# A gated linear recurrence with a maxout FFN: the two tiles of a group come from two sequences instead of two neighbouring stretches of one

## The chip, the core and the metric

The kernel runs on one core of a Trainium2 chip. The core has five engines that work side by side, each with its own queue of instructions: TensorE (PE in the profile, its weight loads PEld), VectorE (DVE), ScalarE (ACT), GpSimd (POOL) and SyncE (SP), which here only issues DMAs. The metric is the device time in microseconds. Before the change it is 688.7 us, the median of three runs (688.65 to 689.51).

## The reference

Four sequences (B = 4) of 768 tokens, with 8 heads of 48 dimensions, go through a recurrence with a complex gate, and then through a feed-forward layer:

```python
mag = np.sqrt(a_re * a_re + a_im * a_im)
scale = np.minimum(mag, 0.999) / (mag + 1e-06)
a_re_n, a_im_n = (a_re * scale, a_im * scale)
...
for t in range(S):
    new_re = ar * S_re - ai * S_im
    new_im = ar * S_im + ai * S_re
    S_re, S_im = (new_re + kv, new_im)
    y[:, :, t] = np.einsum('bhd,bhde->bhe', q[:, :, t], S_re)
...
h = np.maximum(np.maximum(x @ w1, x @ w2), x @ w3)
return (h @ w_out).astype(np.float32)
```

The state S is zero at the start of each sequence, and the sequences do not depend on each other. The FFN works on each of the 3072 tokens by itself (384 to 768 and back). All data are float32.

## The kernel before

**Tiles and groups.** A tile x holds 128 tokens of one sequence, all heads (24 tiles, six per sequence). A group g is C = 2 tiles, which share the work on the gates: 12 groups. Before the change the two tiles of a group are neighbours in one sequence (`GB` = 3 groups per sequence), and tile x follows tile x-1. A tile has two chunks of 64 tokens.

**The gates** (`gate_steps`, `turns`, `sines`, `products`). Instead of running the recurrence token by token, the kernel writes the gate as a size and an angle, sums the logarithms of the size and the angles along the tokens, and multiplies k and q by what the sums give. The step s0 squares (L350, L351) and adds (L352, L353), s1 ends with `Ln`, the logarithm of the size (L362 on ACT, then L363 on DVE), and s2 makes the tangent of half the angle in `w`; L373, on POOL from group 2 on, is one of its products. `turns` takes Arctan of `w` and adds what is missing of the angle (L390, L391). The matmuls `cs` then sum the angles over the tokens of a tile: with the triangular matrix `upto` for the tile's own tokens, and for the second tile of a group also with the matrix of ones `every`, which adds the sum over the first tile. The result is rounded to whole turns (`t`, L403, on ACT) and reduced (`nf`, L405, on DVE), and its cosine and sine (`af`, L419, then `CS`, on ACT) multiply k and q (`uk`, `uq`, L469). The angle at the end of a group is carried to the next: two DMAs on ACT's queue (L413) copy the last row of the second tile's `nf` to the tile `carry`, and in the next group a POOL operation (L381) subtracts it from the first row of `ai`, which L391 adds in. A group at the head of a sequence gets no carry.

**The states.** `state(x)` computes `dk`, the sum of outer products of k and v for both chunks of a tile (32 matmuls, 64 records in the profile, since each float32 matmul has two), and from it the state ahead of the tile's second chunk and ahead of the next tile. The states lie in the tiles `g`, of which there are two. Tile 0 of a sequence has its first state set to zero by POOL (L592) and its second copied from `dk` (L614); elsewhere a state is multiplied by a decay (L616) and `dk` is added (L617). `prep` multiplies k and q by decay factors (L517); its last part makes `QG`, by which the state is read. `scores` makes the products `A` and `B`, `gather` picks from them into `atm` (L564), and `outputs` sums `y` from `atm` and v (inside the chunk) and from `QG` and `g` (from the state ahead of it).

**The FFN.** `up_step` multiplies 256 tokens by a third of the features of one of w1, w2, w3; the first result goes to `hT` by a copy on ACT (L657), the two others by a maximum on DVE (L659). `out_step` multiplies by w_out, and SP's queue stores.

**Order.** All PSUM results use one pool of four tiles (two banks each), handed out as they come free: a new result waits until what was in its tile four results before has been read. Groups 0 and 1 are woven from lists of steps; from group 2 on, `group` calls the steps in an order that is written out, and each matmul is tied to the one before it (`chained`), so that PE's order is that of the source. ACT's activations that need a table are tied to each other in the same way. For everything else the order on an engine is settled when the program is built, by priority and by what is expected to be ready; an engine then works through its queue in that order. In `group(g)` the angles of group g+1 are summed in the middle:

```python
outputs(x, tokens(x))
rest(y)
turning()
pairs(y)
units[0]()
units[1]()
for f in later:
    f()
feed(2)
turned(y + 1)
```

`turning` is `angles` of group g+1, with `feed(2)` inside (two steps of the FFN ahead of the sums); `pairs(y)` is `A`, `B` and their gathers, `units` make `uk` and `uq`, `later` is s0 and s1 of group g+2, and `turned` begins with the transposes `tp`, then `cut` (`F`) and `state` (`dk`).

Of the kernel before, what the change touches and what calls it, by code (L numbers as in the profile page):

```python
# [50 lines left out]
def kernel(  # L51
# [13 lines left out]
    nc = tc.nc  # L65
# [9 lines left out]
    W = C * DM  # L75
    TG = C * P
    NS = S // P
    GB = NS // C
    NG = B * GB
    NX = NG * C  # L80
    HU = 4

# [64 lines left out]
    def ones(name, *shape):  # L147
        t = const.tile([P, *shape], FP, name=name)
        nc.vector.memset(t, 1.0)
        return t  # L150
# [3 lines left out]
        keep(view, -low - 1, [[-s, n] for s, n in lp], 1)  # L154
        keep(view, high, [[s, n] for s, n in hp], -1)

    every = ones("every", L64)

    upto = ones("upto", P)

# [11 lines left out]


    vbs = [const.tile([P, 2, H // 2, P], FP, name="vb%d" % i) for i in range(4)]
    gs = [const.tile([P, 2, H // 2, P], FP, name="g%d" % i) for i in range(2)]
    atms = [const.tile([P, H, L64], FP, name="atm%d" % i) for i in range(2)]

    us = {nm: [const.tile([P, H, 2, L64], FP, name="u%s%d" % (nm, i)) for i in range(n)] for nm, n in (("k", 3), ("q", 2))}
# [56 lines left out]


    def rows(a, g, c, lo=0, n=P):
        b, s = divmod(g, GB)
        t0 = (s * C + c) * P + lo
        return a[b, :, t0:t0 + n, :].rearrange("h t d -> t h d")  # L240

    def load_a(g, c):
        for nm, src in (("ar", a_re), ("ai", a_im)):
# [3 lines left out]

    def halves(a, g, c, j):

        b, s = divmod(g, GB)  # L250
        t0 = (s * C + c) * P
        return a[b, j * 4:(j + 1) * 4, t0:t0 + P, :].rearrange("h (c t) d -> t c h d", c=2)

    def load_kq(g, c):
        for nm, src in (("k", k), ("q", q)):
# [81 lines left out]
    def gate_steps(g, cs):  # L337
        lo, hi = cs[0] * DM, (cs[-1] + 1) * DM

        def part(nm):  # L340
            t = T[nm, g]
            return (flat(t) if len(t.shape) == 4 else t)[:, lo:hi]

        def s0():
            if lo == 0:
                for nm in "Lwe":
                    T[nm, g] = nat1.tile([P, W], FP, tag=nm, name=nm)
                T["Ln", g] = nat2.tile([P, W], FP, tag="Ln", name="Ln")
            L, w, ar, ai = part("L"), part("w"), part("ar"), part("ai")
            nc.scalar.activation(out=w, in_=ar, func=AF.Square)  # L350
            nc.scalar.activation(out=L, in_=ai, func=AF.Square)  # L351
            nc.vector.tensor_tensor(out=L, in0=L, in1=w, op=OP.add)  # L352
            nc.vector.tensor_scalar(out=L, in0=L, scalar1=SMALL, scalar2=LARGE, op0=OP.max, op1=OP.min)  # L353
            act(out=L, in_=L, func=AF.Ln)

        def s1():

            L, w, e = part("L"), part("w"), part("e")
            act(out=w, in_=L, func=AF.Exp, scale=0.5)
            act(out=e, in_=L, func=AF.Exp, scale=-0.5)  # L360
            act(out=e, in_=e, func=AF.Ln, scale=1e-6, bias=1.0)
            nc.scalar.activation(out=L, in_=L, func=AF.Relu, scale=-0.5, bias=lnmax)  # L362
            nc.vector.scalar_tensor_tensor(out=part("Ln"), in0=L, scalar=-LNMAX, in1=e, op0=OP.add, op1=OP.add)  # L363

        def s2():

            L, w, e, ar, ai = part("L"), part("w"), part("e"), part("ar"), part("ai")
            nc.scalar.activation(out=e, in_=ar, func=AF.Abs)
            nc.vector.tensor_tensor(out=w, in0=w, in1=e, op=OP.add)
            act(out=L, in_=w, func=AF.Ln)  # L370
            act(out=L, in_=L, func=AF.Exp, scale=-1.0)

            (nc.gpsimd if g > 1 else nc.vector).tensor_tensor(out=ai, in0=ai, in1=L, op=OP.mult)  # L373
            nc.vector.tensor_tensor(out=w, in0=w, in1=L, op=OP.mult)
            nc.vector.scalar_tensor_tensor(out=w, in0=w, scalar=2.0, in1=ai, op0=OP.subtract, op1=OP.mult)

            nc.scalar.activation(out=ar, in_=ar, func=AF.Sign, bias=tiny)  # L377
            nc.scalar.activation(out=ai, in_=ar, func=AF.Copy, scale=-0.25, bias=0.25)
            nc.scalar.activation(out=ar, in_=ar, func=AF.Copy, scale=-1.0 / math.pi)
            if lo == 0 and g % GB > 0:  # L380
                nc.gpsimd.tensor_tensor(out=ai[0:1, 0:DM], in0=ai[0:1, 0:DM], in1=T["carry", g], op=OP.subtract)  # L381

        return [s0, s1, s2]

    def turns(g, cs, meanwhile):

        lo, hi = cs[0] * DM, (cs[-1] + 1) * DM
        w, ar, ai = T["w", g], flat(T["ar", g]), flat(T["ai", g])
        act(out=w[:, lo:hi], in_=w[:, lo:hi], func=AF.Arctan)
        nc.vector.tensor_tensor(out=w[:, lo:hi], in0=w[:, lo:hi], in1=ar[:, lo:hi], op=OP.mult)  # L390
        nc.vector.tensor_tensor(out=w[:, lo:hi], in0=w[:, lo:hi], in1=ai[:, lo:hi], op=OP.add)  # L391
        meanwhile(2)
        for c in cs:
            ps = banks("cs", DM)

            for ch in range(2):
                for n, mat in enumerate((upto[:, ch * L64:(ch + 1) * L64], every)[0:c + 1]):
                    for j in range(2):
                        at = (c - n) * DM + j * HC
                        mm(out=ps[j * L64:(j + 1) * L64, ch * HC:(ch + 1) * HC], lhsT=mat,  # L400
                           rhs=w[:, at:at + HC], start=n == 0, stop=n == c)
            t = nat2.tile([P, DM], FP, tag="t", name="t")
            nc.scalar.activation(out=t, in_=ps, func=AF.Copy, bias=MAGIC)  # L403
            nf = nat2.tile([P, DM], FP, tag="nf", name="nf")
            nc.vector.scalar_tensor_tensor(out=nf, in0=t, scalar=MAGIC, in1=ps, op0=OP.subtract, op1=OP.subtract)  # L405
            T["nf", g * C + c] = nf
            if g == 0:
                sines(g, [c])
            if c == C - 1 and (g + 1) % GB > 0:
                T["carry", g + 1] = nat1.tile([1, DM], FP, tag="carry", name="carry")  # L410
                for j in range(2):
                    last = (j + 1) * L64
                    nc.scalar.dma_start(out=T["carry", g + 1][:, j * HC:(j + 1) * HC], in_=nf[last - 1:last, HC:])  # L413

    def sines(g, cs):
        for c in cs:
# [94 lines left out]
    def prep(x, part):  # L511
        K, Q, F = T["K", x][0:DD], T["Q", x][0:DD], T["F", x][0:DD]

        def times(out, in_, c, n):

            f = F.rearrange("p s j n -> p (s j) n")[:, :, c:c + n].rearrange("p g (n e) -> p g n e", e=1)
            nc.vector.tensor_tensor(out=out, in0=in_, in1=f.to_broadcast([DD, 2 * H, n, 8]), op=OP.mult)  # L517

        def rows8(t):

            return t.rearrange("p g (n e) -> p g n e", e=8)

        base = Q[:, :, 0:32]
        if part == 0:
            q8 = rows8(Q[:, :, 32:48])
            times(q8, base.rearrange("p g (n u e) -> p g n u e", u=2, e=8)[:, :, :, 1], C8, 4)
            times(q8, q8, C8B, 4)
        elif part == 1:

            times(*(rows8(t.rearrange("p s (j t) -> p (s j) t", j=2)[:, :, 0:48]) for t in (KB[0:DD], K)), CK, 6)  # L530

            QB = un1.tile([P, 2 * H, 96], FP, tag="QB", name="QB")
            T["KB", x], T["QB", x] = KB, QB
            ends = QB[0:DD].rearrange("p g (s u e) -> p g s u e", s=6, e=8)[:, :, 0::5]
            times(ends, rows8(base[:, :, 16:32]), C16, 4)
        elif part == 2:
            src = Q.rearrange("p (g j) t -> p g j t", j=2)[:, :, 1:2, 0:32].to_broadcast([DD, 2 * H, 2, 32])
            times(T["QB", x][0:DD, :, 16:80].rearrange("p g (i n e) -> p g i n e", i=2, e=8),
                  src.rearrange("p g i (n e) -> p g i n e", e=8), C32, 8)
        else:  # L540
            QG = un1.tile([P, 2 * H, L64], FP, tag="QG", name="QG")
            times(rows8(QG[0:DD]), rows8(base), CG, 8)
            T["QG", x] = QG

    def scores(x, nm):
# [40 lines left out]

    def state(x):

        s = x % NS
        T["G", x] = gs[x % 2]  # L590
        if s == 0:
            nc.gpsimd.memset(T["G", x][0:DD, 0], 0.0)  # L592


        ps = banks("dk")
        for n in range(H):
            ch, i = divmod(n, 4)
            for j in range(2):
                r, o = slice(j * L64, (j + 1) * L64), i % 2 * (P - D)
# [9 lines left out]
            return heads(t).rearrange("p (j i) u d -> p j i u d", j=2)  # L609

        for c in range(2 if s < NS - 1 else 1):
            new = four(G[0:DD, 1] if c == 0 else gs[(x + 1) % 2][0:DD, 0])
            if s + c == 0:
                nc.vector.tensor_copy(out=new, in_=dk[:, c])  # L614
                continue
# [3 lines left out]
    def outputs(x, xs):  # L619
# [4 lines left out]
        for r in range(DM // 32):  # L624
            i, w = divmod(r, 3)
            runs = ((0,), (1, 2), (3,))[w]
            for c in range(2):
                todo = [(n, new) for new in (True, False) for n in runs]
                queues[r % 4] += [(r, c, i, n, new, (n, new) == todo[0], (n, new) == todo[-1]) for n, new in todo]
        for todo in zip(*queues):  # L630
            for r, c, i, n, new, start, stop in todo:
# [29 lines left out]
    def out_step(xs, x):  # L661
# [3 lines left out]
            mm(out=ps, lhsT=hT[:, f, o:o + P], rhs=wo[:, f], start=(f == 0), stop=(f == KF - 1))  # L665
        ot = fp2.tile([P, DM], FP, tag="ot", name="ot")
        nc.scalar.copy(out=ot, in_=ps)
        nc.sync.dma_start(out=out[x * P:(x + 1) * P, :], in_=ot)


    def call(f, *a):
# [192 lines left out]
```

## Time and profile before

One execution was profiled. Its time is 688.34 us and the span in the profile 686.6 us.

| what | value |
|---|---|
| time, median of 3 runs | 688.7 us |
| time of the profiled execution, and its span | 688.34 us, 686.6 us |
| mean granted TensorE clock | 0.974 |
| `up` matmuls, busy | 294.3 us |
| `op` matmuls, busy | 98.6 us |
| `y` matmuls, busy | 46.7 and 46.1 us |
| `cs` matmuls with `upto`, with `every`, busy | 22.9 us (192 records), 13.1 us (96) |
| `dk` matmuls, busy | 27.0 us (1536 records) |
| chain of waits, share of PE and of ACT | 69%, 11% |
| carry copies on ACT's queue, issue | 16 of 504 to 1875 ns, median 566 ns; 2.0 to 4.5 us to landing |

How to read it: a busy time is the time in which the engine had an instruction of that group under way. Matmuls overlap, so their rows add up to more than the time they take. In rows by time, the two numbers in front are start and duration, "x12" is the number of records taken together, and what stands in brackets is the idle time of the engine ahead of the instruction with what ended it. "ACTq" is the queue of ACT, which issues DMAs. "L117" is the helper that records every matmul; matmuls are told apart by the tile that they write.

### The profile page before, as it was taken

What the parts mean: (1) busy time and instruction counts of PE and PEld (TensorE: products, weight loads), DVE (VectorE), ACT (ScalarE), POOL (GpSimd) and SP (SyncE); (2) the same over time, 40 slices, a digit from 0 to 9 for tenths busy, and PEclk for the clock granted to TensorE, in tenths of its full rate; (3) what the DMA queues carried; (4) which work ended last, traced back from release to release, by engine and by line L of the source; (5) the groups of instructions that cost most, each with busy time, mean ns of one, the idle gap of its engine ahead of it and who ended that gap; (6) DMA issues with size and microseconds to landing.
All of it is one profiled execution on the core that took longest, in us unless ns stands there. A gap on an engine that the chain in (4) does not pass through costs nothing.

```text
span 686.6 us, 25182 instructions
## 1 busy us (share of the span) xinstructions
PE 613.9 (89%) x11196; PEld 505.9 (74%) x11196; DVE 492.1 (72%) x676; ACT 389.6 (57%) x617; POOL 116.3 (17%) x128
## 2 busy tenths in 40 slices
PE   1263396898999999999999999999999999999997
PEld 0162395887878878878878878878878788887785
DVE  4899898986886787778778777777768768745111
ACT  7788558677565565565755754764854844430000
POOL 9400402304013013013013013013013013000000
PEclk9967799999999999999999999999999999999999
DMA  6684632330330420421420421411410210000000
GB/s 139 205 218 119 176 55 52 61 56 18 70 60 16 75 57 13 82 49 26 75 55 20 78 49 21 81 43 25 82 40 13 48 37 2 3 26 3 12 12 23
DMA packets 138285, 39.41 MB, mean 57 GB/s; under 512 B 130880, under 2 KB 133952, under 8 KB 138176
## 3 DMA queue, kind: packets, MB, share of 16 engines
q1 hardware_dynamic: 137664, 37.78, 24.9%
q8 instruction: 88, 1.44, 0.9%
q14 instruction: 21, 0.17, 0.1%
q10 hardware_dynamic: 512, 0.01, 0.0%
HBM read 33.03 MB, written 4.72 MB: 55 GB/s over the span
## 4 chain that ended last, share of the span: by engine, by line
PE 69%; ACT 11%; issue 7%; DVE 4%; SPq 3%; DMA 3%; POOL 1%; ACTq 1%; POOLq 0%; DVEq 0%
PE up L117 33%; PE op L117 14%; PE y L117 6%; PE tp L117 4%; PE cs L117 3%; PE dk L117 3%; PE B L117 3%; ACT CS L112 2%; PE A L117 2%; ACT e L112 2%; PE sums L117 2%; SPq L259 1%; POOL ai L381 1%; ACT L133 1%; ACT L L112 1%
## 5 line engine op out<-in xcount | busy, mean ns | idle before, releaser
L117 PE MATMUL up<-xT,w 128*128 128x256 f32 (+1 forms) x1404 | 294.3, 367 | 4.7 <-ACT f L112 2.9
L117 PEld LDWEIGHTS up<-xT,w 128*128 128x128 f32 x1404 | 247.5, 190 | 41.5 <-ACT f L112 6.1
L117 PE MATMUL op<-wo,hT 128*128 128x384 f32 x288 | 98.6, 493 | 0.1
L657 ACT COPY hT<-up 128x768 f32<-128x768 f32 (+2 forms) x27 | 19.6, 727 | 121.7 <-PE up L117 121.6
L117 PEld LDWEIGHTS op<-wo,hT 128*128 128x128 f32 x288 | 53.1, 190 | 34.1 <-ACT K L486 0.2
L659 DVE TENSOR_TENSOR hT<-hT,up 128x768 f32<-128x768 f32 (+2 forms) x54 | 46.3, 857 | 44.0 <-PE up L117 43.9
L517 DVE TENSOR_TENSOR Q<-Q,f 112x512 f32<-112x512 f32 x48 | 40.4, 841 | 48.1 <-ACT f L112 48.1
L373 POOL TENSOR_TENSOR ai<-ai,L 128x768 f32<-128x768 f32 x10 | 22.7, 2266 | 295.5 <-ACT L L112 233.2
L517 DVE TENSOR_TENSOR QB<-Q,f 112x512 f32<-112x512 f32 (+1 forms) x48 | 56.9, 1223 | 0.0
L117 PE MATMUL y<-atm,vb 128*32 128x64 f32 x1536 | 46.7, 222 | 0.0
L117 PE MATMUL y<-QG,g 112*32 112x64 f32 x1536 | 46.1, 221 | 0.3 <-issue 0.3
L117 PEld LDWEIGHTS y<-atm,vb 128*32 128x32 f32 x1536 | 39.2, 111 | 9.4 <-ACT ar L377 3.3
L117 PE MATMUL cs<-w,upto 128*64 128x192 f32 x192 | 22.9, 363 | 22.7 <-DVE w L391 22.7
L117 PEld LDWEIGHTS y<-QG,g 112*32 112x32 f32 x1536 | 39.8, 111 | 0.5 <-issue 0.5
L112 ACT ACTIVATE f<-F 48x296 f32<-48x296 f32 x96 | 39.6, 413 | 0.8
L474 DVE TENSOR_TENSOR uk<-uk,En 128x768 f32<-128x768 f32 x24 | 23.5, 979 | 22.5 <-PE tp L117 22.5
L464 POOL TENSOR_TENSOR k<-E,k 128x384 f32<-128x384 f32 x20 | 23.7, 1186 | 81.3 <-ACT E L112 81.3
L117 PE MATMUL B<-QB,KB 112*32 112x80 f32 x1536 | 32.7, 237 | 3.7 <-issue 2.6
L117 PEld LDWEIGHTS cs<-w,upto 128*64 128x64 f32 x192 | 14.4, 151 | 28.4 <-issue 14.9
L117 PE MATMUL sums<-Ln,mid 64*64 64x192 f32 x192 | 14.9, 360 | 22.8 <-DVE Ln L363 22.8
L405 DVE SCALAR_TENSOR_TENSOR nf<-t,cs 128x384 f32<-128x384 f32 x24 | 13.3, 553 | 28.7 <-ACT t L403 28.7
L564 DVE COPY_PREDICATED atm<-masko,B 128x256 f32<-128x256 uint8 x72 | 31.5, 438 | 1.9
(109 smaller groups left out, 1040.9 us busy)
## 6 DMA issues: line engine op xcount, KB each, us to landing
ar<-in_a_re_dram SPq DMA_DIRECT2D x24, 192.0 KB, 4.9
ai<-in_a_im_dram SPq DMA_DIRECT2D x24, 192.0 KB, 3.9
k<-in_k_dram SPq DMA_DIRECT2D x96, 48.0 KB, 2.3
q<-in_q_dram SPq DMA_DIRECT2D x96, 48.0 KB, 2.5
vb<-in_v_dram SPq DMA_DIRECT2D x192, 24.0 KB, 2.2
out_dram<-ot SPq DMA_DIRECT2D x24, 192.0 KB, 1.9
raw<-in_moe_w_dram SPq DMA_DIRECT2D x5, 768.0 KB, 5.6
w<-in_moe_w_dram SPq DMA_DIRECT2D x2, 768.0 KB, 4.6
```

The costliest lines, as they stand in the source:

```text
L112: tab(nc.scalar.activation(**kw))
L117: ins = f(**kw)
L133: tab(nc.scalar.preload_act_table_set(nm))
L259: nc.sync.dma_start(out=t[j * L64:(j + 1) * L64, ch], in_=halves(src, g, c, j)[:, ch])
L373: (nc.gpsimd if g > 1 else nc.vector).tensor_tensor(out=ai, in0=ai, in1=L, op=OP.mult)
L405: nc.vector.scalar_tensor_tensor(out=nf, in0=t, scalar=MAGIC, in1=ps, op0=OP.subtract, op1=OP.subtract)
L464: eng.tensor_tensor(out=hd(T[nm, x]), in0=E, in1=hd(T[nm, x]), op=OP.mult)
L474: nc.vector.tensor_tensor(out=u, in0=u, in1=two(T["En", x]), op=OP.mult)
L517: nc.vector.tensor_tensor(out=out, in0=in_, in1=f.to_broadcast([DD, 2 * H, n, 8]), op=OP.mult)
L564: nc.vector.copy_predicated(out=out, mask=mask, data=data)
L657: nc.scalar.copy(out=dst, in_=ps)
L659: nc.vector.tensor_tensor(out=dst, in0=dst, in1=ps, op=OP.max)
```

## The change

The two tiles of group g are now the same stretch of two sequences: tile x = 2g + c is stretch g mod 6 of sequence 2 (g div 6) + c. The number of groups stays 12, and a pair of sequences takes six groups.

- `every` and its matmuls are gone: each tile sums the angles over its own tokens only.
- The carry has one row for each tile: both tiles copy the last row of their `nf` (four DMAs per group instead of two, in the ten groups that have a successor in their sequence, instead of eight), and L381 subtracts 768 columns instead of 384.
- A state goes from tile x to tile x + 2, so there are four tiles `g`; the first chunk of a sequence gets no state: no memset by POOL, no matmuls with `g` for it in `outputs`, and only the second half of `QG` is made for it.
- The last tile of each sequence computes `dk` for its first chunk only.
- For group 0, Arctan and the two operations behind it run on each tile by itself.
- Loads and stores address the tokens of the new order.

```diff
-    GB = NS // C
-    NG = B * GB
+    NG = B // C * NS
...
-    gs = [const.tile([P, 2, H // 2, P], FP, name="g%d" % i) for i in range(2)]
+    gs = [const.tile([P, 2, H // 2, P], FP, name="g%d" % i) for i in range(4)]
...
-            if lo == 0 and g % GB > 0:
-                nc.gpsimd.tensor_tensor(out=ai[0:1, 0:DM], in0=ai[0:1, 0:DM], in1=T["carry", g], op=OP.subtract)
+            if g % NS > 0:
+                nc.gpsimd.tensor_tensor(out=ai[0:1], in0=ai[0:1], in1=T["carry", g], op=OP.subtract)
...
-        act(out=w[:, lo:hi], in_=w[:, lo:hi], func=AF.Arctan)
-        nc.vector.tensor_tensor(out=w[:, lo:hi], in0=w[:, lo:hi], in1=ar[:, lo:hi], op=OP.mult)
-        nc.vector.tensor_tensor(out=w[:, lo:hi], in0=w[:, lo:hi], in1=ai[:, lo:hi], op=OP.add)
+        for part in [[c] for c in cs] if g == 0 else [cs]:
+            n = slice(part[0] * DM, (part[-1] + 1) * DM)
+            act(out=w[:, n], in_=w[:, n], func=AF.Arctan)
+            nc.vector.tensor_tensor(out=w[:, n], in0=w[:, n], in1=ar[:, n], op=OP.mult)
+            nc.vector.tensor_tensor(out=w[:, n], in0=w[:, n], in1=ai[:, n], op=OP.add)
...
-                for n, mat in enumerate((upto[:, ch * L64:(ch + 1) * L64], every)[0:c + 1]):
-                    for j in range(2):
-                        at = (c - n) * DM + j * HC
-                        mm(out=ps[j * L64:(j + 1) * L64, ch * HC:(ch + 1) * HC], lhsT=mat,
-                           rhs=w[:, at:at + HC], start=n == 0, stop=n == c)
+                for j in range(2):
+                    at = c * DM + j * HC
+                    mm(out=ps[j * L64:(j + 1) * L64, ch * HC:(ch + 1) * HC], lhsT=upto[:, ch * L64:(ch + 1) * L64],
+                       rhs=w[:, at:at + HC], start=True, stop=True)
...
-            if c == C - 1 and (g + 1) % GB > 0:
-                T["carry", g + 1] = nat1.tile([1, DM], FP, tag="carry", name="carry")
+            if (g + 1) % NS > 0:
+                if c == 0:
+                    T["carry", g + 1] = nat1.tile([1, W], FP, tag="carry", name="carry")
                 for j in range(2):
-                    last = (j + 1) * L64
-                    nc.scalar.dma_start(out=T["carry", g + 1][:, j * HC:(j + 1) * HC], in_=nf[last - 1:last, HC:])
+                    last, at = (j + 1) * L64, c * DM + j * HC
+                    nc.scalar.dma_start(out=T["carry", g + 1][:, at:at + HC], in_=nf[last - 1:last, HC:])
...
-            times(rows8(QG[0:DD]), rows8(base), CG, 8)
+            g = 0 if x // C % NS > 0 else H
+            times(rows8(QG[0:DD, g:]), rows8(base[:, 2 * g:]), CG, 8, g)
...
-        s = x % NS
-        T["G", x] = gs[x % 2]
-        if s == 0:
-            nc.gpsimd.memset(T["G", x][0:DD, 0], 0.0)
+        s = x // C % NS
+        T["G", x] = gs[x % 4]
...
-        for n in range(H):
+        for n in range(H if s < NS - 1 else 4):
...
-            new = four(G[0:DD, 1] if c == 0 else gs[(x + 1) % 2][0:DD, 0])
+            new = four(G[0:DD, 1] if c == 0 else gs[(x + C) % 4][0:DD, 0])
...
-                todo = [(n, new) for new in (True, False) for n in runs]
+
+                todo = [(n, new) for new in ((True, False) if x // C % NS > 0 or c > 0 else (True,)) for n in runs]
...
-        nc.sync.dma_start(out=out[x * P:(x + 1) * P, :], in_=ot)
+        t0 = x // C // NS * C * S + x % C * S + x // C % NS * P
+        nc.sync.dma_start(out=out[t0:t0 + P, :], in_=ot)
```

More of the change, by code (lines that the diff above doesn't have):

```diff
@@ L155, in between @@
         keep(view, high, [[s, n] for s, n in hp], -1)
-    every = ones("every", L64)
     upto = ones("upto", P)
@@ L237, in rows @@
     def rows(a, g, c, lo=0, n=P):
-        b, s = divmod(g, GB)
-        t0 = (s * C + c) * P + lo
-        return a[b, :, t0:t0 + n, :].rearrange("h t d -> t h d")
+        b, s = divmod(g, NS)
+        t0 = s * P + lo
+        return a[b * C + c, :, t0:t0 + n, :].rearrange("h t d -> t h d")
     def load_a(g, c):
@@ L248, in halves @@
     def halves(a, g, c, j):
-        b, s = divmod(g, GB)
-        t0 = (s * C + c) * P
-        return a[b, j * 4:(j + 1) * 4, t0:t0 + P, :].rearrange("h (c t) d -> t c h d", c=2)
+        b, s = divmod(g, NS)
+        t0 = s * P
+        return a[b * C + c, j * 4:(j + 1) * 4, t0:t0 + P, :].rearrange("h (c t) d -> t c h d", c=2)
     def load_kq(g, c):
@@ L379, in s2 @@
             nc.scalar.activation(out=ar, in_=ar, func=AF.Copy, scale=-1.0 / math.pi)
-            if lo == 0 and g % GB > 0:
-                nc.gpsimd.tensor_tensor(out=ai[0:1, 0:DM], in0=ai[0:1, 0:DM], in1=T["carry", g], op=OP.subtract)
+            if g % NS > 0:
+                nc.gpsimd.tensor_tensor(out=ai[0:1], in0=ai[0:1], in1=T["carry", g], op=OP.subtract)
         return [s0, s1, s2]
     def turns(g, cs, meanwhile):
-        lo, hi = cs[0] * DM, (cs[-1] + 1) * DM
         w, ar, ai = T["w", g], flat(T["ar", g]), flat(T["ai", g])
-        act(out=w[:, lo:hi], in_=w[:, lo:hi], func=AF.Arctan)
-        nc.vector.tensor_tensor(out=w[:, lo:hi], in0=w[:, lo:hi], in1=ar[:, lo:hi], op=OP.mult)
-        nc.vector.tensor_tensor(out=w[:, lo:hi], in0=w[:, lo:hi], in1=ai[:, lo:hi], op=OP.add)
+        for part in [[c] for c in cs] if g == 0 else [cs]:
[3 more added lines that the diff above has]
+            nc.vector.tensor_tensor(out=w[:, n], in0=w[:, n], in1=ai[:, n], op=OP.add)
         meanwhile(2)
@@ L512, in prep, with times @@
         K, Q, F = T["K", x][0:DD], T["Q", x][0:DD], T["F", x][0:DD]
-        def times(out, in_, c, n):
-            f = F.rearrange("p s j n -> p (s j) n")[:, :, c:c + n].rearrange("p g (n e) -> p g n e", e=1)
-            nc.vector.tensor_tensor(out=out, in0=in_, in1=f.to_broadcast([DD, 2 * H, n, 8]), op=OP.mult)
+        def times(out, in_, c, n, g=0):
+            f = F.rearrange("p s j n -> p (s j) n")[:, g:, c:c + n].rearrange("p g (n e) -> p g n e", e=1)
+            nc.vector.tensor_tensor(out=out, in0=in_, in1=f.to_broadcast([DD, 2 * H - g, n, 8]), op=OP.mult)
         def rows8(t):
```

## The prediction

> **What bounds the kernel now.** I read the busy shares first, then the table of stretches, then one turn of the main loop in order of time.
>
> ```profile
> PE 613.9 (89%) x11196; PEld 505.9 (74%) x11196; DVE 492.1 (72%) x676; ACT 389.6 (57%) x617; POOL 116.3 (17%) x128
> ...
> 50.00:60.00 10.00, 1.21 (x39) 0.92 (x37) 10.00 (x18) 7.56 (x10) 0.00 (x0) 0.70 0.54 131
> 200.00:300.00 100.00, 99.87 (x1849) 82.06 (x1849) 75.95 (x100) 59.57 (x94) 15.52 (x12) 1.00 0.25 51
> ```
>
> The first line gives busy time by engine. In the other two, after the stretch and its length come the busy times of PE, PEld, DVE, ACT and POOL. Up to about 164 us DVE or ACT leads; from there to 650 us PE has work for over 98% of the time, DVE for at most 76%. So what leaves PE after 164 us is worth its time, provided that nothing else then makes PE wait. That is the question, and the section from a group's angle sums (`cs`) to its next `dk` answers it. First a group that copies a carry, then one that does not:
>
> ```profile
> 228.41 1.20 PE L117 MATMUL cs<-w,upto 128*64 128x192 f32 x12
> ...
> 229.44 0.49 PE L117 MATMUL cs<-w,every 128*64 128x192 f32 x4
> ...
> 229.76 0.49 PE L117 MATMUL cs<-w,upto 128*64 128x192 f32 x4
> ...
> 231.74 1.15 ACTq L413 DMA_DIRECT2D carry<-nf  x2
> ...
> 232.94 0.62 ACT L112 ACTIVATE CS<-af,biases 128x384 f32<-128x384 f32 x1 [0.68 <-DVE atm L564]
> ...
> 240.95 0.96 DVE L363 SCALAR_TENSOR_TENSOR Ln<-L,e 128x768 f32<-128x768 f32 x1 [1.56 <-ACT L L362]
> ...
> 241.82 0.95 DVE L659 TENSOR_TENSOR hT<-hT,up 128x768 f32<-128x768 f32 x1
> ...
> 242.83 1.14 PE L117 MATMUL dk<-vb,uk 64*64 64x48 f32 x64
> ```
> ```profile
> 428.78 1.20 PE L117 MATMUL cs<-w,upto 128*64 128x192 f32 x12
> ...
> 440.88 0.95 DVE L659 TENSOR_TENSOR hT<-hT,up 128x768 f32<-128x768 f32 x1 [1.12 <-PE up L117]
> ...
> 442.90 1.11 PE L117 MATMUL dk<-vb,uk 64*64 64x48 f32 x64
> 443.13 0.96 DVE L363 SCALAR_TENSOR_TENSOR Ln<-L,e 128x768 f32<-128x768 f32 x1 [0.41 <-ACT L L362]
> ```
>
> Without a carry, `cs` to `dk` takes 442.90-428.78 = 14.12 us, the same in all three such groups (from 278.53, 428.78, 580.23). With one it takes 14.42 in five groups and 15.70 in the sixth (from 528.76), where one copy's issue took 1.88 us. The lines say why: ACT cannot start `CS` until it has issued two copies, so L362 and DVE's `Ln` come later; the second `hT`, which frees the PSUM tile for `dk`, stands behind `Ln` on DVE. In the other groups the order is `hT`, then `Ln`, and PE waits for nobody. The order is part of the program, fixed when it is built.
>
> **The change, part by part.** The sum is made against the profiled execution, 688.34 us with a span of 686.6; the median shown is 688.7, 0.4 more.
>
> `every`: each group loses 8 of 24 `cs` matmul records. Their busy row (13.1 us) overlaps its neighbours, so I take starts: 229.44 to 229.76 is 0.32 us for four, 0.65 for eight. The nine groups from 178 us on give **-5.85**, if nothing takes the wait's place.
>
> `dk`: half of 64 records go in the last tile of each sequence; 242.83 to 243.97 is 1.14, so 0.57 x 4 = **-2.3**.
>
> `y`: 32 of 128 records go in first tiles; a `y` takes 1.95 in the chain of waits, so 0.49. Two of the four (tiles 12 and 13) lie where PE is full: **-1.0**. The pair in the start is covered by PE's idle time.
>
> Carry copies: 16 become 40, each with a median issue of 0.57 us on ACT's queue, and groups 3, 4 and 6 to 10 make four of them (before: 3, 4, 6, 7, 9, 10, two each). Behind them on ACT stand `CS`, the table load, five gate activations. Second-tile `t` and `nf` come 0.65 earlier; `af` and L350 are handed over by 230.95, four issues end at 233.3, and `CS` starts at about 233.33: 0.4 later than now. `Ln` becomes ready at 241.35, while PE, 0.65 earlier, has finished `up` and made `hT` ready at 239.7. Today these stand 0.6 apart (240.95 against 240.35) and the program takes `Ln` first; without a carry they stand about 2.2 apart and it takes `hT` first. At 1.65 I expect `hT` first, as it is nearer to the second. Then the waits of today go: 5 x 0.30 + 1.58 = **-3.1**; what is late next is PE itself, at 14.12 - 0.65 = 13.47. If the old order stays, the section is 14.42 + 0.4 = 14.82.
>
> [...] The row has 0.57 against 3.9 us to landing, but landing has some 20 us of cover and issue has none: it is 0.30 us of PE per group now. [...] by the row they are free only with `hT` first.
>
> POOL's subtraction grows from 1x384 to 1x768 and happens 10 times, not 8. Two rows:
>
> ```profile
> 71.09 7.71 POOL L381 TENSOR_TENSOR ai<-ai,carry 1x384 f32<-1x384 f32 x1 [46.30 <-ACT ai L378]
> ...
> 118.47 0.99 POOL L381 TENSOR_TENSOR ai<-ai,carry 1x384 f32<-1x384 f32 x1 [2.80 <-ACT ai L378]
> ```
>
> 768 columns cost 2.27 on average at L373, so +1.0 to +1.3 each. In the loop it ends near 257 and `w` L391 reads it at 274.6: covered by 17 us. In group 1 it is on the path: 7.71 us beside a full DVE, ending only after DVE went idle for 0.89. [...] Plain overlap would make it 0; I take +1.0.
>
> The start, to 164 us. `cs` of group 1 runs at a low clock, 0.64 per four: -1.3. That of group 2 gains 0.65 and pays about as much for four new copies on ACT: 0. QG of tiles 0 and 1 halves on DVE (1.21 to about 0.6, DVE over 90% busy): -1.2. Tile 1's state copies (0.55) instead of multiplying and adding (1.3): -0.75. Splitting Arctan and two products for group 0: ACT 0.84 to 2 x 0.51, each product 0.96 to 2 x 0.55: +0.3. Two new copies of group 0 on an ACT 95% busy: 0 to +1.15, taken as +0.4. With POOL: **-1.5**. But there PE's order is not pinned and a rebuilt program may interleave differently; ends -5 and +3.
>
> Nothing for: two memsets (0.27 each at 1.4 us, DVE idle until 5.6), four POOL memsets gone (POOL idle), later halved QGs (DVE has a quarter free), loads and stores of equal size at other addresses, four `g` buffers (a wait fewer).
>
> Sum: 5.85 + 2.3 + 1.0 + 3.1 + 1.5 = 13.7; 688.34 - 13.7 = 674.6, or **675.0** beside the median.
>
> **Rivals.** (a) *The old order stays*, `Ln` before `hT`. Groups 3, 4, 6, 7, 9: +0.4 each; group 8: 14.82 - 14.12 = +0.7; group 10: -0.9; groups 5 and 11: -0.65 each. Net +0.5 in place of -8.95: 684.0, **684.5** by the median. For it: six groups do so now. Against: the distance grows. (b) *`A` holds PE*. The list of waits names `nf` as releaser of `A`'s weight load nine times (2.5 us in all). If `A` cannot start before the first tile's `nf`, which does not move, `cs` gains nothing: 13.7 - 5.85, **680.9**. Against: PSUM tiles go round by four, so `A` takes the one of the last `up` but one, and `cs` shows the same 0.3 us gap with no releaser. (c) *Slower: the copies go ahead of `af` on ACT*, as the source has them. Issues from 230.43 to 232.75, then `af` 0.42 and L350 0.85: `CS` at 234.02, 1.08 late, section 15.50 with `Ln` first. That is 5 x 1.08 - 0.2 + 1.4 - 1.3 = +5.3; less 3.3 for `dk` and `y`, and with the start at +1 for the same reason: **691.7**. With the start at -1.5 it tips when the carry sections pass 15.4 us. Against: ACT's order now puts `af` first, and such lateness makes `hT` first likelier. (d) The start's new order eats the gain, near 688.
>
> **Numbers.** Forecast 0.50, (a) 0.22, (b) 0.13, (c) 0.09, (d) 0.06. The forecast's own ends are 671 to 678 (start -5 to +2); the range to 685.5 takes in (a) and (b) and leaves out (c), (d) and the far tails. About 0.2%, 1.4 us, is what a measurement tells from no change. Faster: the forecast, (a), (b), 0.85. Same 0.05, slower 0.10.
>
> **What would show it.** `cs` with 16 records in some 1.45 us; `dk` about 13.5 us after `cs` in all nine groups, with `hT` ahead of `Ln`: the forecast. 14.8 in seven groups and 13.5 in two, `dk` released by `hT`: (a). A gap ahead of `A` that brings it to 2.1 us after `cs` starts: (b). ACTq L413 ahead of `af`: (c). The first `cs` at full PE (178.3 now) should come 1 to 2 us earlier; later than 181 breaks the start's sum.

## The result, and the profile after

The changed kernel takes 678.6 us (median; 677.9 to 678.9), the kernel before, run beside it, 688.9: a ratio of 0.9848, with a 95% interval of 0.983 to 0.9865. That is 10.3 us faster and 3.6 short of the forecast. It lies inside the range to 685.5, just above the forecast's own ends of 671 to 678. The profiled execution has a span of 676.8 us where the one before had 686.6.

The busy times and the clock of the page, and two stretches of the table that the prediction showed:

```profile
PE 609.0 (90%) x10844; PEld 500.3 (74%) x10844; DVE 499.4 (74%) x679; ACT 388.9 (57%) x618; POOL 125.4 (19%) x126
...
PEclk9977697899999999999999999999999999999999
```
```profile
50.00:60.00 10.00, 4.11 (x111) 3.42 (x109) 10.00 (x20) 8.14 (x10) 0.00 (x0) 0.84 0.56 129
200.00:300.00 100.00, 99.87 (x1860) 81.69 (x1849) 80.62 (x101) 61.56 (x98) 21.16 (x13) 1.00 0.28 54
```

PE has 352 matmul records fewer and is as full between 200 and 300 us as it was: the loop is still bound by PE, and whatever left it there was worth its time. The same section as in the prediction, one group with carry copies, in order of time:

```profile
228.88 1.52 PE L116 MATMUL cs<-w,upto 128*64 128x192 f32 x16
230.33 0.89 PE L116 MATMUL A<-Q,K 112*32 112x48 f32 x64
...
230.91 3.29 ACTq L412 DMA_DIRECT2D carry<-nf  x4
...
234.25 0.94 ACT L418 ACTIVATE af<-nf 128x384 f32<-128x384 f32 x2 [2.58 <-DMA carry<-nf]
...
239.67 2.01 DVE L658 TENSOR_TENSOR hT<-hT,up 128x768 f32<-128x768 f32 x2
...
241.57 0.92 ACT L360 ACTIVATE L<-L,biases 128x768 f32<-128x768 f32 x1
...
242.35 1.11 PE L116 MATMUL dk<-vb,uk 64*64 64x48 f32 x64
...
242.40 0.99 ACT L485 COPY K<-tp 112x1024 f32<-112x1024 f32 x1
...
242.52 0.96 DVE L361 SCALAR_TENSOR_TENSOR Ln<-L,e 128x768 f32<-128x768 f32 x1 [0.84 <-ACT L L360]
...
243.52 0.85 ACT L366 ACTIVATE e<-ar 128x768 f32<-128x768 f32 x1
```

`A` starts 1.45 us after `cs`, not 2.10, and `dk` 13.47 us after it, in all nine groups from 178 us on. `hT` now stands ahead of `Ln`, and `dk` waits for nobody. But the four copies have gone ahead of `af` on ACT, the place that rival (c) gave them: in this group `CS` starts 6.21 us after `cs` where it was 4.53. And ACT's row has changed too: the eviction of `K` (L485) stands ahead of the Abs (L366), which stood ahead of `K` before. This last exchange was in nobody's sum. The lines of the kernel before that show these places, in the group that starts at 228.41:

```profile
230.51 0.89 PE L117 MATMUL A<-Q,K 112*32 112x48 f32 x64
...
231.02 0.52 ACT L419 ACTIVATE af<-nf 128x384 f32<-128x384 f32 x1
...
241.94 0.84 ACT L368 ACTIVATE e<-ar 128x768 f32<-128x768 f32 x1 [1.02 <-DVE Ln L363]
242.69 0.99 ACT L486 COPY K<-tp 112x1024 f32<-112x1024 f32 x1
```

The start is where the trace disagrees with the forecast. Its lines, first PE and then the two others:

```profile
79.72 2.83 PE L116 MATMUL cs<-w,upto 128*64 128x192 f32 x16 [8.04 <-DVE w L390]
...
105.41 0.89 PE L116 MATMUL A<-Q,K 112*32 112x48 f32 x64 [2.54 <-DVE Q L516]
...
109.34 5.98 PE L116 MATMUL op<-wo,hT 128*128 128x384 f32 x12
```
```profile
71.20 7.38 POOL L379 TENSOR_TENSOR ai<-ai,carry 1x768 f32<-1x768 f32 x1 [46.52 <-ACT ai L376]
...
78.61 0.96 DVE L390 TENSOR_TENSOR w<-w,ai 128x768 f32<-128x768 f32 x1 [1.69 <-POOL ai L379]
```

Before, the last of these lines and that of `op` were:

```profile
78.83 0.96 DVE L391 TENSOR_TENSOR w<-w,ai 128x768 f32<-128x768 f32 x1 [0.89 <-POOL ai L381]
...
109.94 4.14 PE L117 MATMUL op<-wo,hT 128*128 128x384 f32 x12
```

The add of `ai` to `w` waits 1.69 us for POOL where it was 0.89, and `op` takes 5.98 us for the same twelve records. At 106.26, between `A` and `op`, the clock granted to TensorE fell to half. The first `cs` at full PE comes at 179.72, 1.42 us later than before and not 1.5 sooner.

The table that the rest of this text uses has one row per profiled execution, built from the starts of `cs`: group 0 to group 1, group 1 to group 3, and from there to the end of the span. The last column is the ratio of times to the kernel before on the same chip.

| kernel | g0 to g1 | g1 to g3 | g3 to end | ratio |
|---|---|---|---|---|
| before | 52.75 | 98.36 | 508.3 | 1 |
| before_hT_first | 52.73 | 99.64 | 508.2 | 1.0018 |
| before_hT_K_first | 52.32 | 100.90 | 504.2 | 0.9965 |
| changed | 53.64 | 100.00 | 497.1 | 0.9848 |
| after_again (the changed kernel) | 53.64 | 100.15 | 497.8 | 0.984 |
| after_every_back | 53.61 | 100.44 | 502.2 | 0.9919 |
| after_Ln_first | 53.63 | 98.25 | 503.2 | 0.9926 |
| after_Ln_first_copies_last | 53.62 | 97.69 | 496.4 | 0.9831 |
| after_fill | 53.62 | 101.82 | 497.8 | 0.9903 |
| after_fill2 | 53.61 | 99.39 | 497.2 | 0.9834 |
| after_fill3 | 53.63 | 98.37 | 497.1 | 0.9836 |
| after_fill01 | 53.63 | 97.71 | 497.1 | 0.9818 |
| after_carry_dve | 52.83 | 100.29 | 497.0 | 0.9821 |
| after_best | 52.82 | 97.21 | 496.7 | 0.9795 |

### The profile page after: what moved, and what is told of

Read it like the earlier page. It is cut to its first block, busy times and chain, and to the rows that moved or that the text cites. A ratio compares the mean times of both kernels' runs of the same rounds, so it can differ in the third digit from the quotient of the medians.

```text
span 676.8 us, 24522 instructions
## 1 busy us (share of the span) xinstructions
PE 609.0 (90%) x10844; PEld 500.3 (74%) x10844; DVE 499.4 (74%) x679; ACT 388.9 (57%) x618; POOL 125.4 (19%) x126
## 4 chain that ended last, share of the span: by engine, by line
PE 76%; ACT 10%; DVE 7%; DMA 3%; issue 2%; POOL 1%; SPq 1%; DVEq 0%; ACTq 0%; POOLq 0%
PE up L116 40%; PE op L116 14%; PE y L116 6%; PE tp L116 5%; PE B L116 4%; PE A L116 2%; PE cs L116 2%; PE dk L116 2%; ACT f L111 2%; PE sums L116 1%; PE F L116 1%; POOL ai L379 1%; ACT Q L489 1%; DVE Q L516 1%; DMA w<-in_moe_w_dram 1%
## 5 line engine op out<-in xcount | busy, mean ns | idle before, releaser
L116 PE MATMUL up<-xT,w 128*128 128x256 f32 (+1 forms) x1404 | 297.6, 370 | 6.0 <-ACT f L111 3.0
L116 PEld LDWEIGHTS up<-xT,w 128*128 128x128 f32 x1404 | 250.5, 193 | 43.0 <-ACT f L111 6.3
L116 PE MATMUL op<-wo,hT 128*128 128x384 f32 x288 | 100.4, 500 | 0.1
L516 DVE TENSOR_TENSOR QB<-Q,f 112x512 f32<-112x512 f32 (+1 forms) x48 | 61.1, 1309 | 0.0
L116 PE MATMUL y<-QG,g 112*32 112x64 f32 x1408 | 44.3, 222 | 0.2 <-DVE g L612 0.2
L379 POOL TENSOR_TENSOR ai<-ai,carry 1x768 f32<-1x768 f32 x10 | 24.5, 2448 | 86.6 <-ACT ai L376 77.7
L116 PEld LDWEIGHTS y<-QG,g 112*32 112x32 f32 x1408 | 37.9, 112 | 0.4 <-DVE g L612 0.4
L116 PE MATMUL cs<-w,upto 128*64 128x192 f32 x192 | 20.9, 366 | 18.2 <-DVE w L390 18.2
L116 PEld LDWEIGHTS A<-Q,K 112*32 112x32 f32 x1536 | 18.9, 112 | 19.2 <-issue 9.4
```

The lines of the kernel that those rows point to most:

```text
L116: ins = f(**kw)
L379: nc.gpsimd.tensor_tensor(out=ai[0:1], in0=ai[0:1], in1=T["carry", g], op=OP.subtract)
```

## The experiments

A program rebuilt after an edit may order its instructions anew. In all of them except after_Ln_first the order of DVE and ACT was therefore held to that of the kernel compared with, by dependencies that order and do not wait, with the exchanges named and no others.

### The order of hT and Ln, in the kernel before

In six groups DVE's row `hT, Ln, hT` becomes `hT, hT, Ln`; nothing else moves.

```
-hT  Ln  hT
+hT  hT  Ln
```

> The kernel before, in which only one thing moves: in the six groups where VectorE's row had hT, Ln, hT, the row is now hT, hT, Ln (the rest of every engine's row is pinned to what it was). Theory (the two orders are what the 3.1 us of carry waits hung on): all nine sections from cs to dk become 14.12, the six that were 14.42 (five) and 15.70 (one) lose 3.1 us, the total goes from 688.9 to 685.8. Rival (the waits only change their name, because the work behind Ln is late in its turn): 688.9, within 0.3.

The ratio was 1.0018 (1.0006 to 1.003). All nine sections did come to 14.12 us, 3.0 us less in all, but the time from `dk` to the next `cs` grew by 3.7. ACT and PE of that kernel in the group that starts at 231.12 (a helper records all of DVE's and ACT's instructions there, so they share line L76):

```profile
244.09 0.95 DVE L76 SCALAR_TENSOR_TENSOR Ln<-L,e 128x768 f32<-128x768 f32 x1
...
245.08 0.84 ACT L76 ACTIVATE e<-ar 128x768 f32<-128x768 f32 x1 [1.45 <-DVE Ln L76]
...
245.83 0.99 ACT L76 COPY K<-tp 112x1024 f32<-112x1024 f32 x1
...
246.87 0.91 PE L138 MATMUL op<-wo,hT 128*128 128x384 f32 x2 [0.52 <-ACT K L76]
```

And the list of waits (engine, instruction and releaser; then us in total, times, and the longest):

```profile
PE op L138 <- ACT K L76: 3.5, 6, 0.9
```

The Abs overwrites `e`, which `Ln` reads. With `Ln` later, Abs waits for it, the eviction of `K` waits behind Abs, and `op` waits for the PSUM tile that `K` frees. The rival held in kind: the wait had only changed its name, and by 0.2% the new one costs more than the old. Hence the second run:

```
 DVE  -hT  Ln  hT      ACT  -Abs (e<-ar)  K
      +hT  hT  Ln           +K  Abs (e<-ar)
```

> The kernel before with two exchanges in each of the six carry groups: hT ahead of Ln on VectorE (as in the run before_hT_first) and, new, the eviction of K ahead of the Abs of ar on ScalarE. That run had turned the six waits of dk into six waits of op for K (0.52 us): Abs overwrites e, which Ln reads, so it waits for the later Ln, and K stood behind it. Theory (the 3.1 us need both exchanges, and the changed kernel has both): cs to dk 14.12 and cs to cs about 49.8 in all groups, total 3.1 us under before, ratio 0.9955. Rival (the wait moves on once more, to Q or F behind Abs): no change, ratio 1.000 to 1.002.

The ratio was 0.9965 (0.9951 to 0.9979), 2.4 us. From the `cs` of group 3 to that of group 11 it took 398.6 us against 401.9: 3.3 us by the trace, where 3.1 was expected. So the carry waits are worth what the prediction said. The exchange of `hT` and `Ln` alone doesn't save them, both exchanges do, and the changed kernel has both.

### The matmuls of `every`

A matrix of zeros takes the place of `every` in the second tile's angle sums, from group 3 on; what is computed stays the same.

```
-                    mm(..., lhsT=upto[...], rhs=w[:, at:at + HC], start=True, stop=True)
+                n_mat = c + 1 if g > 2 else 1
+                for n, mat in enumerate((upto[...], every)[0:n_mat]):
...
+                        mm(..., lhsT=mat, rhs=w[:, at:at + HC], start=n == 0, stop=n == n_mat - 1)
```

> The kernel after, with the matmuls of a matrix of zeros put back into the second tile's angle sums from group 3 on (36 instructions in nine groups), all orders of VectorE and ScalarE pinned to those of the kernel after. Theory (TensorE is the bound in this stretch, each group's share is 0.65 us): cs to A 2.10 instead of 1.45, cs to dk 14.12 instead of 13.47, total 678.6 + 5.85 = 684.4. Rival (part of the gain came from VectorE's new order, not from the matmuls): the sections stay under 14.0 and the total under 683.

The ratio was 0.9919 (0.9894 to 0.9944), 684.1 us: 5.5 over the changed kernel by the medians, 4.9 by the ratios. PE of that kernel, one group:

```profile
231.10 1.20 PE L137 MATMUL cs<-w,upto 128*64 128x192 f32 x12
232.13 0.49 PE L137 MATMUL cs<-w,every 128*64 128x192 f32 x4
232.45 0.49 PE L137 MATMUL cs<-w,upto 128*64 128x192 f32 x4
232.78 0.49 PE L137 MATMUL cs<-w,every 128*64 128x192 f32 x4
233.20 0.89 PE L137 MATMUL A<-Q,K 112*32 112x48 f32 x64
```

`A` is back at 2.10 and `dk` at 14.12 in all nine groups. The eight `cs` to `cs` grew by 5.0 us together, 0.63 each. This part of the gain is PE's own work. Rival (b) is out: in the changed kernel nothing held `A` back to 2.10.

### The old order, and the copies' place, in the changed kernel

First DVE's row alone goes back; then also the copies move behind the last `CS` of their group on ACT.

```
-hT  hT  Ln
+hT  Ln  hT
```

> The kernel after, in which only VectorE's order goes back: hT, Ln, hT in the groups from 2 to 9. The copies still stand ahead of af on ScalarE, so CS ends about 1.7 us later than in the kernel before and Ln with it. Theory (the copies would cost their place in the row if hT stood behind Ln, rival of the third kind in the prediction): the second hT ends about 2.1 us later than TensorE needs its bank, the section is about 15.5 in the seven groups that carry, total 678.6 + 7 x 2.1 = 693, slower than the kernel before. Other theory (the place of Ln is worth nothing now): 678.6.

```
 DVE  -hT  hT  Ln      ACT  -carry x4  af  af  CS  CS  CS  CS
      +hT  Ln  hT           +af  af  CS  CS  CS  CS  carry x4
```

> The changed kernel with VectorE's old order (hT, Ln, hT) in its seven carry groups, as in after_Ln_first, but with the four carry copies of each group behind the last CS on ScalarE instead of ahead of af. In after_Ln_first these groups were 0.2 to 1.3 us longer from cs to dk, 6.0 us in all. Theory (that price was the copies' place): the sections come to 13.47 plus at most the 0.30 us of the kernel before, total at most 2.1 us over the changed kernel, near 680. Rival (the old order costs that much wherever the copies stand): 6 us over it, near 684.

The first came to 0.9926 (0.9907 to 0.9946), 683.7 us, the second to 0.9831 (0.9815 to 0.9848), 677.7. The same group in the first and then in the second kernel:

```profile
380.20 3.52 ACTq L412 DMA_DIRECT2D carry<-nf  x4
...
383.76 0.94 ACT L418 ACTIVATE af<-nf 128x384 f32<-128x384 f32 x2 [2.80 <-DMA carry<-nf]
...
392.04 0.96 DVE L361 SCALAR_TENSOR_TENSOR Ln<-L,e 128x768 f32<-128x768 f32 x1 [1.90 <-ACT L L360]
392.92 0.95 DVE L658 TENSOR_TENSOR hT<-hT,up 128x768 f32<-128x768 f32 x1
...
392.96 1.14 PE L116 MATMUL dk<-vb,uk 64*64 64x48 f32 x64 [1.13 <-ACT K L485]
```
```profile
377.59 0.93 ACT L418 ACTIVATE af<-nf 128x384 f32<-128x384 f32 x2
...
386.64 0.96 DVE L361 SCALAR_TENSOR_TENSOR Ln<-L,e 128x768 f32<-128x768 f32 x1 [0.72 <-ACT L L360]
387.52 0.94 DVE L658 TENSOR_TENSOR hT<-hT,up 128x768 f32<-128x768 f32 x1
...
388.37 1.11 PE L116 MATMUL dk<-vb,uk 64*64 64x48 f32 x64
```

With the copies ahead of `af`, the old order costs 0.24 to 1.31 us in the seven carry groups, 6.0 together; with the copies behind `CS` all nine sections are 13.47. So the theory of the second run held: the price is the copies' place. Its size was missed in the first run, 0.86 a group and not 2.1. In that trace `dk` waits for `K`, which stands behind the copies on ACT too, and starts while the second `hT` still runs: in this rebuilt program `dk` must have another PSUM tile, so it isn't the wait of the kernel before made longer. In the second run `dk` starts 0.09 us before the second `hT` ends and doesn't wait for that one either. The changed kernel pays nothing for the copies, since its `dk` waits neither for `K` nor for an `hT` behind the `Ln` that they delay. That the copies last and the old order would cost nothing is shown only for a program in which `dk` doesn't need the PSUM tile of the second `hT`.

### The start: clock or order?

The same program again, for a second trace:

> The changed kernel once more, as the baseline of this call and for a second trace. Ratio to before 0.985. Theory (the dips of TensorE's clock in the start depend on where the idle stretches fall in that one execution): the time from the cs of group 1 to that of group 2, 52.19 in the first trace and 49.64 and 51.75 in two kernels with the same start, comes out at another value between 49.5 and 52.5, with a clock row to match. Rival (the lateness is in the new order of work): 52.2 again whatever the clock row shows.

The ratio was 0.984 (0.9817 to 0.9862). Group 1 to group 2 took 51.51 us after 52.19; in the kernels above with the same start up to there it was 51.75 and 49.64, in three executions of the start of before 50.46, 50.99 and 52.61. So a single trace doesn't tell the start to better than about 1.3 us either way, and the difference to before that the profiled pair shows in groups 1 to 3, 1.64 us, isn't one that I can claim. The first `cs` at full PE came at 181.41 this time, past the 181 at which the prediction gave its own sum up. The 0.9 us from group 0 to group 1 is steady: 52.3 to 52.8 in the three of before, 53.6 in every trace of the changed start.

Then fillers: matmuls of constants into a PSUM tile that nobody reads, where PE is idle.

```
+    def fill(n):
+        idle = banks("idle", P)
+        for _ in range(n):
...
+            mm(out=idle, lhsT=upto, rhs=ident, start=True, stop=True)
...
```

> The kernel after, with 40 matmuls of constants [...] between the y of tile 1 and the A of tile 2, where TensorE was idle for 2.54 us; all else pinned. Theory (the idle stretch takes TensorE's clock down to half, and the start lost its time to that): the granted clock stays at 1.00 from 106 to 113, the op of that place takes 4.0 instead of 5.8 us, the first cs of the loop comes 1.8 us sooner or more, total 676.8 or a little less. Rival (the start is late because of the new order of VectorE and POOL, the clock merely follows): 678.6 or later, within 0.4.

The ratio was 0.9903 (0.9887 to 0.9919). The filler was sized wrongly: one of its f32 matmuls is two records of 0.115 us, and 40 of them took 9.2 us in a gap of 2.5. `A` came 5.6 us later, yet group 1 to group 2 lost 1.8 us and not 5.6: `op` took 4.1 us at full clock, and `B` ahead of it no longer waited for DVE. This decides nothing; the next sizes follow from it.

> The changed kernel with two fillers of TensorE of the right length this time (a 128x128 f32 matmul costs 0.23 us, 40 of them took 9.2 us in the run after_fill): 10 between the y of tile 1 and the A of tile 2, 9 ahead of the up that waits 2.16 us for f. All else pinned. Theory (clock): full clock from 86 on, cs of group 1 to cs of group 2 at 49.5, 1.5 to 2.7 us less than the changed kernel, ratio to it 0.997. Rival (order of work): no gain, ratio to it 1.000 or above.

> As after_fill2, with a third filler of 28 matmuls (6.4 us) in the 8.0 us in which TensorE waits for w ahead of the cs of group 1, behind which cs and up ran at half clock for 5.9 us. Theory (clock): the clock stays full through 80 to 86, the A of tile 1 comes up to 2.9 us sooner, of which VectorE's and ScalarE's work beside it lets about half through: 1.5 us less than after_fill2, a total near 674.5 where the changed kernel has 678.6. Rival (the stretch is bound by VectorE): the same as after_fill2.

They came to 0.9834 (0.9812 to 0.9856) and 0.9836 (0.9812 to 0.9859), no gain that can be told from 0.984. PE of after_fill3 shows why:

```profile
118.94 3.62 PE L116 MATMUL idle<-ident,upto 128*128 128x128 f32 x18 [2.21 <-ACT f L111]
122.36 2.50 PE L116 MATMUL up<-xT,w 128*128 128x128 f32 x18
```

The filler ahead of `up` had to wait for the PSUM tile for which `up` itself had waited, and then pushed `up` back by its own length, 3.4 us at a clock that fell at 119.61: its 18 records took 3.62 us, where the 56 of the filler ahead of `cs` took 6.42. It gave away what the others had brought. Without it:

> The changed kernel with two fillers of TensorE: 28 matmuls ahead of the cs of group 1 and 10 between the y of tile 1 and the A of tile 2; the third one of after_fill3 is left out, because there it had to wait for the PSUM tile that the up behind it had been waiting for, and pushed that up from about 40.0 to 42.3 us after the cs of group 1. Theory (the clock's dips in the start do cost time, after_fill3 gave its gain back through its third filler): up at 40.0, the cs of group 2 at 48.5 to 49.6 after that of group 1 (50.89 in after_fill3, 51.5 to 52.2 in the changed kernel), total 1.3 to 2.4 us under after_fill3, near 676. Rival (the start is bound by other engines, the clock costs nothing): 50.9 to 52 again, total 678.

The ratio was 0.9818 (0.9803 to 0.9833). In a table of stretches the granted clock is the third number from the end of a row; the first pair of rows is the changed kernel, the second after_fill01:

```profile
80.00:86.00 6.00, 6.00 (x33) 5.12 (x31) 5.37 (x11) 2.95 (x5) 0.00 (x0) 0.52 0.54 154
106.00:114.00 8.00, 7.24 (x100) 4.92 (x89) 7.52 (x11) 5.08 (x6) 1.17 (x1) 0.57 0.11 17
```
```profile
80.00:86.00 6.00, 5.53 (x52) 5.28 (x52) 5.87 (x12) 2.67 (x5) 0.00 (x0) 1.00 0.53 149
106.00:114.00 8.00, 7.88 (x158) 5.95 (x162) 7.83 (x12) 5.04 (x7) 2.10 (x1) 1.00 0.27 60
```

Half clock, or nearly so, has become full clock in both. Group 1 to group 2 took 48.83 us, in the band that the clock theory gave and below all seven executions of the two starts without fillers; `up` came 38.9 us after the `cs` of group 1, where it was at 42.3. With the same fillers after_best, below, took 48.43. Up to group 3 the gain is less clear: 97.71 us against 98.25 to 100.44 in the four of the changed start, but also 97.69 in after_Ln_first_copies_last, which has no filler. In the total this is 0.2% under 0.984, with intervals that overlap.

### The subtraction of the carry in group 1

```
-                nc.gpsimd.tensor_tensor(out=ai[0:1], in0=ai[0:1], in1=T["carry", g], op=OP.subtract)
+                (nc.vector if g == 1 else nc.gpsimd).tensor_tensor(out=ai[0:1], ...)
```

> The changed kernel with the carry subtraction of group 1 alone moved from POOL, where it took 7.38 us from 71.2 on, to VectorE, right ahead of the add of ai to w that waited 1.69 us for it. Theory (all of the stage from the cs of group 0 to that of group 1 that is longer than before, 53.6 against 52.7, is this wait): the wait goes, the instruction costs about 0.9 us on VectorE, cs to cs comes to 52.9, total 0.7 us less than the changed kernel. Rival (VectorE has other work to catch up there): no gain.

The ratio was 0.9821 (0.9807 to 0.9836), which overlaps with 0.984; the trace is plainer. DVE of that kernel:

```profile
77.05 0.94 DVE L379 TENSOR_TENSOR ai<-ai,carry 1x768 f32<-1x768 f32 x1
78.02 0.96 DVE L390 TENSOR_TENSOR w<-w,ai 128x768 f32<-128x768 f32 x1
```

The wait is gone, and group 0 to group 1 takes 52.83 us, the time of before. The steady part of the start's loss is this wait.

### A version that beats both

> Both together, after_fill01 and after_carry_dve. If both theories hold, the sum of both: 2 to 3 us under the changed kernel, ratio to before 0.980 to 0.981. If neither, the changed kernel's 0.9845.

after_best takes 675.7 us (674.0 to 676.7), a ratio of 0.9795 (0.9777 to 0.9814). The interval lies below both of the changed kernel, 0.983 to 0.9865 and 0.9817 to 0.9862. Its trace has both gains, 52.82 us and 97.21 us in the table.

## Why the prediction was right in sign and 3.6 us off

**`every`, -5.85: right.** 0.65 us in each of nine groups by the starts of `A`, 0.63 from `cs` to `cs` when put back.

**Carry waits, -3.1: right in size, its reason incomplete.** The nine sections together shrank by 8.90 us, 8.95 were predicted for this and `every`. The step said that `hT` ahead of `Ln` makes the waits go. Run alone, that exchange gained nothing; it takes `K` ahead of Abs as well. The forecast didn't ask what else reads or overwrites `Ln`'s inputs. The rebuilt program made both exchanges; the forecast got that by luck. Its ground for `hT` first wasn't met as stated either: `Ln` became ready 2.2 us behind `hT` in the group shown and not 1.65, as the copies had gone ahead of `af`. Why the build chose these orders is not shown.

**The copies' place: wrong, and without effect.** The copies were to stand after `af` and make `CS` 0.4 us later. They stand ahead of it, the place of rival (c), and in the group shown `CS` is 1.7 later. Rival (c) priced this together with the old order at 691.7; those two together ran at 683.7. That this is close to the 684.5 of (a), the old order alone, is chance: there `dk` was to wait for `hT`, and it waited for `K`. That the copies' issue has a price on ACT, as the prediction read from its row, the runs bear out: with the copies ahead of `af` and `Ln` first, they cost 6.0 us. The row's own "only with `hT` first" was too narrow, as they cost nothing behind `CS` either: the nine sections are 13.47 us there too.

**`dk`, -2.3: mis-sized.** 1.14 us was the length of the row of 64 records, ends included. By starts, `dk` to the next instruction went from 0.84 to 0.39 for one tile and from about 1.06 to 0.59 for the other three: -1.86.

**`y`, -1.0: half of it.** Tile 13 went from 1.95 to 1.49. Tile 12 went from 1.94 to 1.86 only, as the `up` behind it then waits 0.30 us for DVE to free a PSUM tile of `dk` (`g` L615): a wait that took the place of the work.

**The start, -1.5: wrong; +1.4 in the profiled pair.** One term was right: the carry on POOL was taken as +1.0 and measured +0.9. The wait of `w` grew by 0.80, and after DVE had gone idle the subtraction needed 0.89 us before and 1.69 now, near the 1.04 and 1.86 (medians) that it takes in the loop, though it had been under way for 6.85 and 5.7 us in which DVE was busy without a pause. Why it took so long beside DVE is not shown; plain overlap would have hidden the 0.80.

Three terms failed. `cs` of group 1 was mis-sized at -1.3. It did become 1.29 us shorter, but `A` of the same tile came 8.53 us after its start, before 8.61: half clock lasted 6.1 us from there and not 4.8, and the `up` between them took 5.85 us in place of 4.64. Where half clock lasted equally long, 4.81 us in the trace of before and 4.83 in after_again, `A` came after 8.61 and 7.95: by these traces the term is worth -0.66. The 1.95 us for QG and state copies were worth nothing: from the `A` of tile 1 to `F` it is 12.11 us in both kernels, and from `F` to the next `A` 5.04. They were counted because DVE was over 90% busy; but in the changed kernel the last wait ahead of that `A` runs from PE's `F` over ACT's `f` to DVE's `Q`, and DVE stood idle for `f`, 1.52 us before and 0.44 after. Freed DVE time was no freed path.

What remains is the clock: kept full in the two stretches shown, it is worth about 2.4 us between groups 1 and 2 (48.83 in one trace against a mean of 51.27 in four executions of the changed start), and without fillers this time moves by 2 to 2.5 us from one execution to the next. How much of the 1.4 us is the change and how much this spread stays open, except for the 0.9 of POOL. The medians give an estimate: they fell by 10.3 us and the time from group 3 on by 11.2, so the start would cost about 0.9 more than before, give or take the 1.2 us of the ratio's interval.

The span shrank by 9.8 us where the sum had 13.7: of the 3.9 missing, 2.9 lie in the start and 0.9 in `dk` and `y`; the rest of the loop was within 0.2. The forecast's own ends counted the start up to +2 where its paragraph had +3; with that they reach 679.5 and take in the 678.6.

## What to carry to other kernels

A wait that goes by an exchange in one engine's row must be followed into the next engine: ask what overwrites the data that the delayed instruction reads, and what is queued behind that writer. In the start, where the granted clock was 0.52 and 0.57 in the two stretches shown, busy shares did not name the bound: in such a place follow the last wait, and count a saving only if it lies on that chain. Put the issue of small transfers behind the work that others wait for: here that removed the cost of 6.0 us which they had in one of the two orders of DVE's row.

## What the hardware did that I had not expected

In the changed kernel's trace TensorE's clock fell to half behind idle stretches of 2.54 us (ahead of `A`, at 106.26) and 2.16 us (ahead of `up`, from 123.33 to 126.74). In the trace before the same 2.16 us ahead of `up` left it full. Where 6.74 us of matmuls filled the 8.0 us gap ahead of the `cs` of group 1, the clock from 80 to 86 us was 1.00 (after_fill01) and not 0.52 (the changed kernel).

Why the same gap did it once and not the other time is not shown. In the changed kernel's trace the clock changed at 106.26, 113.09, 123.33 and 126.74, so that half clock lasted 6.83 us behind the first gap and 3.41 behind the second. The two pairs of rows below put the stretch that holds most of the 2.16 us ahead of the one that follows, first in the changed kernel and then before (PE's busy time is the second number, the clock the third from the end). In the first row of each pair PE had no matmul for 2.07 us in the changed kernel and for 1.86 before, and the clock behind it was 0.50 in the one and 1.00 in the other:

```profile
119.91:123.33 3.42, 1.35 (x12) 1.35 (x13) 1.77 (x3) 3.36 (x9) 2.02 (x2) 1.00 0.02 2
123.33:126.74 3.41, 3.41 (x78) 3.19 (x80) 3.41 (x4) 1.65 (x4) 3.41 (x3) 0.50 0.03 5
```
```profile
118.88:122.30 3.42, 1.56 (x14) 1.56 (x15) 1.77 (x4) 3.36 (x8) 1.21 (x2) 1.00 0.00 0
122.30:125.71 3.41, 3.41 (x142) 3.20 (x141) 3.41 (x3) 1.65 (x4) 3.41 (x3) 1.00 0.07 12
```

These are two traces; the fillers closed gaps, but no run moved one by a few tenths of a microsecond to see what the clock does.

In the changed kernel's trace POOL's subtraction of one row of 768 took 7.38 us in the start, in the first 5.7 of which DVE was never idle, and 1.86 (median of all ten); on DVE the same instruction took 0.94 (after_carry_dve).

Four copies of 192 elements, issued one after the other on ACT's queue, held the next ACT instruction for 2.58 us in the group of the changed kernel shown above.
